# Pooling sums one unit at a time instead of two, under another list of departures from the planner's rule

## The chip, the cores and the metric

The kernel runs on one core of a Trainium2 chip. The metric is the device time of one execution in microseconds. Three runs of the kernel before gave 328.3, 327.56 and 328.4 us; the median is 328.3. Engines are named as in the profile: PE is TensorE (matrix products), DVE is VectorE, ACT is ScalarE, POOL is GpSimd, SP is the queue that issues most of the transfers.

## The reference

`x` has 4 batches of 12544 rows of 128 numbers; `inducing` has 32 rows of 128. Two attention steps are followed by a maxout layer:

```python
def mab(q, kv):
    s = scale * (q @ kv.transpose(0, 2, 1))
    s = s - s.max(-1, keepdims=True)
    a = np.exp(s)
    a /= a.sum(-1, keepdims=True) + 1e-09
    return a @ kv
h = mab(I, x)                      # 32 pooled rows for each batch
y = mab(x, h).reshape(B * S, D)    # every row of x attends to the 32 pooled rows
h1, h2 = y @ w1, y @ w2            # 128 -> 1024, twice
out = np.maximum(h1, h2) @ w_out   # 1024 -> 128
```

## The kernel before

A batch is cut into 98 chunks of 128 rows. The kernel never forms `y`. Since `max(h1, h2) = h1 + relu(h2 - h1)`, and `y` is a softmax row times the 32 pooled rows `h`, it folds the weights into them once for each batch: `hwd = h (w2 - w1)` (32 x 1024) and `m1`, which is `h w1 w_out` with the kernel's sign (32 x 128). For every chunk the main part then does this:

- `stage` (line 591) forms the exponentials `e` of up to 16 chunks in column tiles of TensorE (four tiles of 32 columns); ScalarE takes the exp.
- A `phase` (line 978) multiplies `e` with `hwd` in row tiles (four tiles of 32 rows). It fills up to four PSUM banks. Each bank is brought to SBUF through a relu, on ScalarE (line 994) or VectorE (line 997). In place of one of the four it can hold the linear part with `m1`.
- `final_one` (line 801) is one full 128 x 128 product of a relu piece with `w_out`. A phase of four banks feeds sixteen of them. The finished group is scaled by the reciprocal of the softmax sum (line 828) and stored (line 853).

So TensorE goes back and forth between row tiles, the full array and column tiles.

Beside this the pooled rows of batches 1 to 3 are prepared while the batch before is in its main part (batch 0 is pooled in a first part of its own). The pooling takes the 98 chunks as six units of 16 and a rest of two. For each unit:

- `pool_scores` (line 308), in column tiles, gives scores of 512 columns; ScalarE takes the exp with a running sum into one column of the tile `es` (line 319).
- `pool_turn` (line 345) transposes the exponentials by a transfer on SP's queue.
- `pool_accum` (line 364), in column tiles, multiplies them with the rows of x; VectorE brings the 128 x 128 partial sum to the tile `hacc` (lines 395 and 397).

In the kernel before `pool_accum` is called for every second unit: 32 products of two units stand in one bank, and VectorE adds once. In the last call the rest of two chunks is added in the same bank (line 383), with products with a column of ones that put the rest's sum of exponentials in column 128; VectorE has reduced `es` into column 128 of `hacc` beforehand (line 357), so the last add completes both the sums of rows and the sum of E. Then follow

- `small_rep` (line 409): one fp32 product of the 128 x 129 tile with `repd`, which adds the four column tiles and repeats the result; VectorE takes the reciprocal of column 128 (line 412) and scales (line 414) into the f16 tile `h4`.
- `small_h` (line 439): an f16 transpose of `h4`, copied to `hT4` (line 441).
- `small_hwd` (line 473) and `small_m1` (line 493), which fold the weights.

After the last `pool_accum` of a batch POOL copies a number that depends on the finished sum (`pace`, line 164) and then issues the seven loads of the next batch's rows.

The order of all instructions is fixed when the kernel is built. A planner keeps an account of when TensorE, ScalarE and VectorE are free (`Clock`: costs such as `ck.run(0.49, "col")` or `ck.on_dve(end, 0.22)`) and of when each of the eight PSUM banks is free. At each step it takes side work, column work, a phase or one output product. The small jobs carry a due time in finished chunks (`at`) and a condition (`ready`). The list `DEV` names steps at which the planner departs from its rule: 1 puts a phase off by one product, 2 takes a phase sooner, 3 takes no column work before a phase at this step, 4 takes column work sooner. If the account foresees that TensorE would wait, `keep_busy` puts in products without effect (line 758).

Of the kernel before, what the change touches and what calls it, by code (L numbers as in the profile page):

```python
# [102 lines left out]
def kernel(  # L103
# [56 lines left out]
    def load_x(b, i, after=None):  # L160
        k0, n = parts[b][i]
        if after is not None:

            nc.gpsimd.tensor_copy(out=pace, in_=after)  # L164
        nc.gpsimd.dma_start(out=xn_at[b, i][:, 0:n, :], in_=xr[b, :, k0 : k0 + n, :])  # L165
# [31 lines left out]
    with tc.manual_schedule(engines={ET.PE, ET.DVE, ET.Activation, ET.Pool, ET.SP}):  # L197
# [99 lines left out]
        def xn_of(b, k):  # L297
            for i, (k0, n) in enumerate(parts[b]):
                if k0 <= k < k0 + n:
                    return xn_at[b, i][:, k - k0, :]  # L300

        def pool_scores(b, u):
            if u == 0:
                st[b]["es"] = smp.tile([128, NU], F32, name=f"es_{b}", tag="esu")
            bi, ps = bank([128, 512])
            ck.wait(ck.bank[bi], "p1")
            for g in range(4):
                nc.tensor.matmul(  # L308
                    out=ps[32 * g : 32 * (g + 1), :],
                    lhsT=inducingT,  # L310
                    rhs=xT_tiles[b % 2][:, U * u + 4 * g : U * u + 4 * (g + 1), :],
                    start=True,
                    stop=True,
                    tile_position=(0, 32 * g),
                    skip_group_check=True,
                )
            end = ck.run(0.226, "col")
            eu = etp.tile([128, 512], F16, name=f"eu_{b}_{u}", tag="eu", bufs=NEU)
            nc.scalar.activation(  # L319
                out=eu, in_=ps, func=AF.Exp, scale=scale, accum_out=st[b]["es"][:, u : u + 1]  # L320
            )
            ck.bank[bi] = ck.on_act(end, 0.65)
            st[b]["eu", u] = eu, ck.bank[bi]
# [22 lines left out]
            st[b]["eT", u] = eT, ck.pe  # L346

        def pool_accum(b, u):

            bi, ps = bank([128, 512])  # L350
            ck.wait(ck.bank[bi], "p1")
            last = u == NU - 1
            if u == 1:
                st[b]["hacc"] = smp.tile([128, C + 1], F32, name=f"hacc_{b}", tag="hacc")
            acc = st[b]["hacc"]
            if last:
                nc.vector.reduce_sum(out=acc[:, C : C + 1], in_=st[b]["es"], axis=AX.X)
                ck.on_dve(st[b]["eu", u][1], 0.1)
            for v in (u - 1, u):
                eT = st[b]["eT", v][0]  # L360
                st[b]["sum", v] = True
                for j in range(4):
                    for g in range(4):
                        nc.tensor.matmul(  # L364
                            out=ps[32 * g : 32 * (g + 1), 0:128],
                            lhsT=eT[:, j, 32 * g : 32 * (g + 1)],
                            rhs=xn_of(b, U * v + 4 * g + j),
                            start=(j == 0 and v < u),
                            stop=(j == 3 and v == u and not (last and g < REST)),
                            tile_position=(0, 32 * g),  # L370
                            skip_group_check=True,
                        )
            if last:
                et = st[b]["et"][0]
                for g in range(4):
                    pairs = [(warm[:, 0:M], ones16[:, 0:1], 128, 1)]
                    if g < REST:
                        pairs = [
                            (et[:, g, :], xn_of(b, U * NU + g), 0, 128),
                            (et[:, g, :], ones16[:, 0:1], 128, 1),  # L380
                        ]
                    for lhsT, rhs, lo, n in pairs:
                        nc.tensor.matmul(
                            out=ps[32 * g : 32 * (g + 1), lo : lo + n],
                            lhsT=lhsT,
                            rhs=rhs,
                            start=False,
                            stop=True,
                            tile_position=(0, 32 * g),
                            skip_group_check=True,  # L390
                        )
            end = ck.run(0.58 if last else 0.49, "col")
            n = C + 1 if last else C
            if u == 1:
                nc.vector.tensor_copy(out=acc[:, 0:n], in_=ps[:, 0:n])
            else:
                nc.vector.tensor_add(out=acc[:, 0:n], in0=ps[:, 0:n], in1=acc[:, 0:n])  # L397
            ck.bank[bi] = ck.on_dve(end, 0.22)
            if last:
                st[b]["esrr"] = ck.bank[bi]  # L400
            if last and b + 1 < B:
                for i in range(7):
                    load_x(b + 1, i, acc[:, C : C + 1] if i == 0 else None)

        def small_rep(b):

            bi, ps = bank([128, 512])
            ck.wait(ck.bank[bi], "p1")
            nc.tensor.matmul(out=ps[:, 0 : C + 1], lhsT=repd, rhs=st[b]["hacc"], start=True, stop=True)  # L409
            end = ck.run(0.28)  # L410
            rec = smp.tile([128, 1], F32, name=f"rec_{b}", tag="rec")
            nc.vector.reciprocal(out=rec, in_=ps[:, C : C + 1])
            h4 = smp.tile([128, C], F16, name=f"h4_{b}", tag="h4")
            nc.vector.tensor_scalar(out=h4, in0=ps[:, 0:C], scalar1=rec, scalar2=None, op0=ALU.mult)
            st[b]["h4"] = h4
            ck.bank[bi] = st[b]["haccr"] = ck.on_dve(end, 0.45)

        def small_h(b):
            hT4 = smp.tile([C, 4, M], F16, name=f"hT4_{b}", tag="hT4")
            if b == 0:  # L420


                nc.vector.tensor_scalar(
                    out=hT4,
                    in0=st[0]["hps"][:, None, 0:M].broadcast_to((C, 4, M)),
                    scalar1=DOWN,
                    scalar2=None,
                    op0=ALU.mult,
                )
                st[b]["hT4r"] = ck.on_dve(st[0]["end"], 0.3)  # L430
                ck.bank[st[0]["hb"]] = st[b]["hT4r"]
                es = smp.tile([128, 1], F32, name="es_0", tag="es")
                nc.scalar.copy(out=es, in_=st[0]["eps"][:, 0:1])
                ready = ck.on_act(st[0]["end"], 0.2)
                st[b]["hT4"] = hT4.rearrange("c q m -> c (q m)")
                return es, ready
            bi, ps = bank([128, 128], F16)
            ck.wait(ck.bank[bi], "p1")
            nc.tensor.transpose(ps[:, 0:128], st[b]["h4"], identity16)
            end = ck.run(0.056)  # L440
            nc.vector.tensor_copy(out=hT4.rearrange("c q m -> c (q m)"), in_=ps[:, 0:128])
            ck.bank[bi] = st[b]["hT4r"] = ck.on_dve(end, 0.2)
            st[b]["hT4"] = hT4.rearrange("c q m -> c (q m)")
# [434 lines left out]
        def want_linear():  # L878
# [12 lines left out]


        DEV = {
            31: 1, 54: 1, 107: 2, 141: 1, 148: 1, 177: 4, 201: 1, 231: 1, 268: 1, 285: 1, 289: 1, 297: 2,
            308: 3, 310: 4, 331: 1, 339: 4, 357: 4, 358: 4, 366: 1, 375: 1, 397: 1, 409: 1, 446: 3, 457: 1,
            463: 4, 465: 3, 488: 1, 518: 2, 542: 3, 567: 4, 612: 3, 653: 1, 752: 1, 805: 1, 810: 2, 829: 1,
            834: 4, 842: 1, 846: 1, 863: 1, 900: 1, 920: 4, 946: 1, 950: 1, 966: 1, 1005: 1, 1025: 1, 1050:
            2, 1111: 1, 1119: 1, 1138: 1, 1152: 1, 1163: 1, 1190: 1, 1201: 1, 1282: 1, 1294: 1, 1299: 1,
            1301: 4, 1349: 4, 1362: 3, 1363: 2, 1370: 4, 1379: 1, 1396: 2, 1435: 1, 1459: 1, 1469: 1, 1472:
            3, 1519: 1, 1534: 1, 1536: 3, 1543: 4, 1572: 3, 1606: 1, 1617: 4, 1635: 1, 1654: 3, 1686: 1,  # L900
            1701: 3, 1729: 1
        }
        LIMIT = -16

# [107 lines left out]
        for b in range(1, B):  # L1012
            base = DONE0[b - 1]
            t_first, t_step = (6, 2.2) if b == 1 else (-6, 3.4)
            for u in range(NU):
                if b == 1:
                    s, turn, acc = 25 + 5 * u, 45 + 1.5 * u, 55 + 2 * u
                else:
                    s = turn = 13 + 8.2 * u
                    acc = s + 12  # L1020
                at(base + int(s), pool_scores, b, u)
                at(base + int(turn), pool_turn, b, u)
                if u % 2:
                    at(base + int(acc), pool_accum, b, u)
            s, end = int(s), base + int(acc)
            at(base + s + 2, pool_rest, b)
            at(end, small_rep, b)
# [165 lines left out]
```

## Time and profile before

| | |
|---|---|
| median of three runs | 328.3 us |
| the profiled execution | 328.3 us |
| its span, first to last instruction | 326.2 us |
| PE busy | 320.8 us, 5404 products |
| DVE busy | 282.3 us |
| ACT busy | 281.8 us |
| POOL busy | 25.4 us |
| output products (line 801) | 217.9 us, 3136 products |
| phases (line 978) | 88.7 + 38.8 us in two groups, 1261 products |
| pooling sums (line 364) | 5.5 us, 288 products |
| small_rep (line 409) | 1.3 us, 3 products of two passes each |

Busy time is the union of an engine's instructions; matmuls overlap, so the mean of one is longer than the distance to the next. The first 32 us or so are the first part (loading, pooling of batch 0, folding of its weights); the main part takes nearly all the rest.

### The profile page before, as it was taken

The page shows a single profiled execution, that of the slowest core. Times are in us where ns is not written, and L with a number is a line of the kernel's source. Part 1 is how long each engine was busy: PE and PEld are TensorE (multiplying, and loading weights), DVE is VectorE, ACT ScalarE, POOL GpSimd, SP SyncE. Part 2 cuts the span into 40 slices and gives each one's busy share as a digit, 9 for nine tenths or more (in the row PEclk, how much of TensorE's full clock was granted, in tenths as well). Part 3 has the DMA queues.
Part 4 walks back from the last instruction along what each step waited for, and adds up shares of the span by engine and source line. Part 5 has one row for each costly group of instructions (what it writes and reads, how often), then busy time and mean ns, then how long its engine had stood idle before and what let it go on. Part 6 is the DMA issues. An engine that isn't in the chain of part 4 may idle for free.

```text
span 326.2 us, 12587 instructions
## 1 busy us (share of the span) xinstructions
PE 320.8 (98%) x5404; PEld 243.0 (74%) x5404; DVE 282.3 (87%) x518; ACT 281.8 (86%) x564; POOL 25.4 (8%) x51
## 2 busy tenths in 40 slices
PE   8999999999999999999999999999999999999996
PEld 3886777677777777777777777777777777778785
DVE  2459998998989999999989989898999999989873
ACT  3679899999978999999988999899979999999961
POOL 7351030000040000000040000000000000000000
PEclk9999999999999999999999999999999999999999
DMA  8999999954289999983479999992422212222233
GB/s 206 209 205 213 289 235 210 228 157 131 98 170 243 191 271 200 196 180 120 111 137 239 219 254 211 191 199 81 133 97 96 86 66 100 98 98 98 87 112 112
DMA packets 70823, 53.65 MB, mean 164 GB/s; under 512 B 52176, under 2 KB 55408, under 8 KB 70768
## 3 DMA queue, kind: packets, MB, share of 16 engines
q1 hardware_dynamic: 64656, 38.63, 49.1%
q0 software_dynamic: 6112, 14.22, 22.3%
q8 instruction: 42, 0.69, 0.9%
q14 instruction: 13, 0.11, 0.1%
HBM read 28.33 MB, written 25.69 MB: 166 GB/s over the span
## 4 chain that ended last, share of the span: by engine, by line
PE 98%; ACT 0%; issue 0%; DVE 0%; ACTq 0%
PE ps L801 61%; PE ps L978 23%; PE ps L591 3%; PE ps L232 2%; PE ps L364 1%; PE ps L308 1%; PE ps L657 1%; PE ps L248 1%; PE ps L280 1%; PE ps L631 1%; PE ps L649 1%; PE ps L758 1%; PE ps L271 1%; PE ps L473 0%; PE ps L409 0%
## 5 line engine op out<-in xcount | busy, mean ns | idle before, releaser
L994 ACT ACTIVATE relu<-ps 128x512 f16<-128x512 f32 x465 | 245.3, 605 | 25.3 <-PE ps L978 16.2
L997 DVE TENSOR_SCALAR relu<-ps 128x512 f16<-128x512 f32 x319 | 204.9, 682 | 19.8 <-PE ps L978 18.3
L801 PE MATMUL ps<-woutp,relu 128*128 128x128 f16 x3136 | 217.9, 220 | 0.1
L801 PEld LDWEIGHTS <-relu 128*128 128x128 f16 x3136 | 177.0, 98 | 40.7 <-issue 30.1
L978 PE MATMUL ps<-e,hwd 32*128 32x512 f16 (+2 forms) x880 | 88.7, 360 | 0.0
L828 DVE TENSOR_TENSOR o<-ps,rp 128x512 f32<-128x512 f32 (+3 forms) x108 | 68.5, 634 | 5.7 <-PE ps L801 3.4
L978 PEld LDWEIGHTS <-hwd 32*128 32x128 f16 x880 | 24.6, 91 | 20.9 <-issue 0.8
L978 PE MATMUL ps<-m,e 32*128 32x128 f16 x381 | 38.8, 217 | 0.0
L978 PEld LDWEIGHTS <-e 32*128 32x128 f16 x381 | 21.3, 92 | 2.6
L165 POOL DMA_DIRECT2D xn<-in_x_dram x31 | 16.7, 551 | 8.4 <-DMA xn<-in_x_dram 4.5
L236 DVE COPY xT<-ps 128x512 f16<-128x512 f16 (+3 forms) x11 | 5.5, 504 | 8.2 <-PE ps L232 8.1
L603 ACT ACTIVATE e<-ps 128x512 f16<-128x512 f32 (+2 forms) x21 | 11.6, 570 | 0.0
L319 ACT ACTIVATE eu<-ps 128x512 f16<-128x512 f32 x18 | 10.8, 617 | 0.0
L591 PE MATMUL ps<-xT,hT 128*32 128x512 f16 (+3 forms) x114 | 10.1, 366 | 0.0
L164 POOL COPY pace<-hacc 128x1 f32<-128x1 f32 x2 | 0.4, 183 | 116.2 <-DVE hacc L397 116.2
L239 ACT COPY xT<-ps 128x768 f16<-128x768 f16 (+3 forms) x11 | 6.1, 556 | 3.5 <-PE ps L232 3.3
L232 PE MATMUL ps<-identity,xn 128*128 128x128 f16 x98 | 7.8, 226 | 0.1
L232 PEld LDWEIGHTS <-xn 128*128 128x128 f16 x98 | 6.0, 101 | 1.5 <-DVE xn L653 0.9
L257 ACT ACTIVATE et<-ps 128x448 f16<-128x448 f32 (+4 forms) x11 | 4.5, 413 | 2.6 <-PE ps L248 2.6
L641 DVE RECIPROCAL rp<-ps 128x16 f32<-128x16 f32 (+2 forms) x28 | 6.7, 239 | 0.0
L631 PE MATMUL ps<-ones_q,e 128*128 128x4 f16 x102 | 6.6, 166 | 0.0
L591 PEld LDWEIGHTS <-hT 128*32 128x32 f16 x114 | 2.6, 93 | 5.1 <-issue 4.2
(96 smaller groups left out, 112.6 us busy)
## 6 DMA issues: line engine op xcount, KB each, us to landing
out_dram<-o SPq DMA_DIRECT2D x90, 256.0 KB, 2.5
xn<-in_x_dram POOLq DMA_DIRECT2D x24, 448.0 KB, 12.0
out_dram<-o SPq DMA_DIRECT2D x10, 128.0 KB, 3.4
xn<-in_moe_w_dram POOLq DMA_DIRECT2D x4, 256.0 KB, 13.8
xn<-in_x_dram POOLq DMA_DIRECT2D x4, 224.0 KB, 10.2
xT<-xn SPq DMA_TRANSPOSE x42, 3.6
xf<-in_x_dram SPq DMA_DIRECT2D x1, 512.0 KB, 3.6
xf<-in_x_dram SPq DMA_DIRECT2D x1, 384.0 KB, 4.0
```

Of the source, the lines that this page charges most:

```text
L165: nc.gpsimd.dma_start(out=xn_at[b, i][:, 0:n, :], in_=xr[b, :, k0 : k0 + n, :])
L232: nc.tensor.transpose(ps[:, j, :], xn[:, g + j, :], identity16)
L319: nc.scalar.activation(out=eu, in_=ps, func=AF.Exp, scale=scale, accum_out=st[b]["es"][:, u : u + 1])
L591: nc.tensor.matmul(out=ps[32 * q : 32 * (q + 1), 128 * t : 128 * (t + n)], lhsT=hq, rhs=xT[:, c : c + n, :], start=True, stop=True, tile_p ...
L603: nc.scalar.activation(out=blk.e2[:, 0 : 128 * wd], in_=ps[:, 0 : 128 * wd], func=AF.Exp, scale=st[0]["rs"] if blk.b == 0 else scale,)
L631: nc.tensor.matmul(out=ps[:, 4 * t : 4 * t + 4], lhsT=blk.e2[:, 128 * t : 128 * (t + 1)], rhs=ones_q, start=True, stop=True,)
L641: nc.vector.reciprocal(out=blk.rp[:, 0:wd, :].rearrange("p t q -> p (t q)"), in_=ps[:, 0 : 4 * wd])
L801: nc.tensor.matmul(out=g.ps[:, 128 * c : 128 * (c + 1)], lhsT=g.blk.relu[q][:, 128 * (jb * w4 + t) : 128 * (jb * w4 + t + 1)], rhs=woutp[: ...
L828: nc.vector.tensor_mul(osb[:, 0:n, :], g.ps[:, 0 : n * C].rearrange("p (s c) -> p s c", s=n), rp)
L978: nc.tensor.matmul(**seq[i])
L994: nc.scalar.activation(out=dst, in_=src, func=AF.Relu)
L997: nc.vector.tensor_scalar(out=dst, in0=src, scalar1=0.0, scalar2=None, op0=ALU.max)
```

## The change

Three things change together.

First, `pool_accum` is called for every unit: 16 products, one bank, and one copy or add on VectorE each, so 18 calls in place of 9. Each is booked in the planner's account with 0.26 us of TensorE and 0.2 of VectorE.

Second, the sum of E is kept apart from the sums of rows. `es` gets a seventh column and is cleared by POOL. The rest's sum is copied from the bank into it on 64 partitions, and only then `es` is reduced into a new tile `esr`. `small_rep` multiplies only this one column with `repd`; VectorE takes the reciprocal and scales `hacc` in place, in fp32. `small_h` is an fp32 product of `hacc` with `repd`, which adds the four column tiles and transposes in one. The products of a column of ones with the cleared tile `warm` go.

Third, `DEV` lists 84 steps in place of 81, at other places.

```diff
         def pool_scores(b, u):
             if u == 0:
-                st[b]["es"] = smp.tile([128, NU], F32, name=f"es_{b}", tag="esu")
+                st[b]["es"] = smp.tile([128, NU + 1], F32, name=f"es_{b}", tag="esu")
+                nc.gpsimd.memset(st[b]["es"], 0.0)
...
         def pool_accum(b, u):
-
             bi, ps = bank([128, 512])
             ck.wait(ck.bank[bi], "p1")
+            eT = st[b]["eT", u][0]
+            st[b]["sum", u] = True
             last = u == NU - 1
-            if u == 1:
-                st[b]["hacc"] = smp.tile([128, C + 1], F32, name=f"hacc_{b}", tag="hacc")
-            acc = st[b]["hacc"]
-            if last:
-                nc.vector.reduce_sum(out=acc[:, C : C + 1], in_=st[b]["es"], axis=AX.X)
-                ck.on_dve(st[b]["eu", u][1], 0.1)
-            for v in (u - 1, u):
-                eT = st[b]["eT", v][0]
-                st[b]["sum", v] = True
-                for j in range(4):
-                    for g in range(4):
-                        nc.tensor.matmul(
-                            out=ps[32 * g : 32 * (g + 1), 0:128],
-                            lhsT=eT[:, j, 32 * g : 32 * (g + 1)],
-                            rhs=xn_of(b, U * v + 4 * g + j),
...
+            for j in range(4):
+                for g in range(4):
+                    nc.tensor.matmul(
+                        out=ps[32 * g : 32 * (g + 1), 0:128],
+                        lhsT=eT[:, j, 32 * g : 32 * (g + 1)],
+                        rhs=xn_of(b, U * u + 4 * g + j),
+                        start=(j == 0),
+                        stop=(j == 3 and not (last and g < REST)),
...
             if last:
                 et = st[b]["et"][0]
-                for g in range(4):
-                    pairs = [(warm[:, 0:M], ones16[:, 0:1], 128, 1)]
...
+                for g in range(REST):
+                    for rhs, lo, n in ((xn_of(b, U * NU + g), 0, 128), (ones16[:, 0:1], 128, 1)):
...
-            end = ck.run(0.58 if last else 0.49, "col")
-            n = C + 1 if last else C
-            if u == 1:
-                nc.vector.tensor_copy(out=acc[:, 0:n], in_=ps[:, 0:n])
+            end = ck.run(0.26, "col")
+            if u == 0:
+                st[b]["hacc"] = smp.tile([128, C], F32, name=f"hacc_{b}", tag="hacc")
+                nc.vector.tensor_copy(out=st[b]["hacc"], in_=ps[:, 0:128])
             else:
-                nc.vector.tensor_add(out=acc[:, 0:n], in0=ps[:, 0:n], in1=acc[:, 0:n])
-            ck.bank[bi] = ck.on_dve(end, 0.22)
+                acc = st[b]["hacc"]
+                nc.vector.tensor_add(out=acc, in0=ps[:, 0:128], in1=acc)
+            ck.bank[bi] = ck.on_dve(end, 0.2)
             if last:
-                st[b]["esrr"] = ck.bank[bi]
-            if last and b + 1 < B:
-                for i in range(7):
-                    load_x(b + 1, i, acc[:, C : C + 1] if i == 0 else None)
+                es = st[b]["es"]
+                nc.vector.tensor_copy(out=es[0 : 32 * REST, NU : NU + 1], in_=ps[0 : 32 * REST, 128:129])
+                esr = smp.tile([128, 1], F32, name=f"esr_{b}", tag="esr")
+                nc.vector.reduce_sum(out=esr, in_=es, axis=AX.X)
+                st[b]["esr"] = esr
+                ck.bank[bi] = st[b]["esrr"] = ck.on_dve(end, 0.2)
+                if b + 1 < B:
+                    for i in range(7):
+                        load_x(b + 1, i, esr if i == 0 else None)
 
         def small_rep(b):
-            nc.tensor.matmul(out=ps[:, 0 : C + 1], lhsT=repd, rhs=st[b]["hacc"], start=True, stop=True)
-            end = ck.run(0.28)
+            nc.tensor.matmul(out=ps[:, 0:1], lhsT=repd, rhs=st[b]["esr"], start=True, stop=True)
+            end = ck.run(0.11)
...
-            nc.vector.reciprocal(out=rec, in_=ps[:, C : C + 1])
-            h4 = smp.tile([128, C], F16, name=f"h4_{b}", tag="h4")
-            nc.vector.tensor_scalar(out=h4, in0=ps[:, 0:C], scalar1=rec, scalar2=None, op0=ALU.mult)
-            st[b]["h4"] = h4
-            ck.bank[bi] = st[b]["haccr"] = ck.on_dve(end, 0.45)
+            nc.vector.reciprocal(out=rec, in_=ps[:, 0:1])
+            acc = st[b]["hacc"]
+            nc.vector.tensor_scalar(out=acc, in0=acc, scalar1=rec, scalar2=None, op0=ALU.mult)
+            ck.bank[bi] = st[b]["haccr"] = ck.on_dve(end, 0.4)
 
         def small_h(b):
...
-            bi, ps = bank([128, 128], F16)
+            bi, ps = bank([128, 512])
             ck.wait(ck.bank[bi], "p1")
-            nc.tensor.transpose(ps[:, 0:128], st[b]["h4"], identity16)
-            end = ck.run(0.056)
+            nc.tensor.matmul(out=ps[:, 0:128], lhsT=st[b]["hacc"], rhs=repd, start=True, stop=True)
+            end = ck.run(0.25)
             nc.vector.tensor_copy(out=hT4.rearrange("c q m -> c (q m)"), in_=ps[:, 0:128])
...
         DEV = {
-            31: 1, 54: 1, 107: 2, 141: 1, 148: 1, 177: 4, 201: 1, 231: 1, 268: 1, 285: 1, 289: 1, 297: 2,
...
+            0: 1, 27: 1, 32: 1, 35: 2, 52: 1, 87: 2, 157: 3, 168: 1, 169: 4, 181: 2, 244: 2, 247: 1, 397: 4,
...
                 at(base + int(s), pool_scores, b, u)
                 at(base + int(turn), pool_turn, b, u)
-                if u % 2:
-                    at(base + int(acc), pool_accum, b, u)
+                at(base + int(acc), pool_accum, b, u)
```

## The prediction

> **What bounds the kernel now.** I read the page first: busy shares, chain that ended last, groups; then the order of the instructions of both programs; then what each engine waited for; then stretches of the main part; then single moments around the pooling.
>
> ```profile
> PE 320.8 (98%) x5404; PEld 243.0 (74%) x5404; DVE 282.3 (87%) x518; ACT 281.8 (86%) x564; POOL 25.4 (8%) x51
> ...
> PEclk9999999999999999999999999999999999999999
> ...
> PE 98%; ACT 0%; issue 0%; DVE 0%; ACTq 0%
> ...
> L994 ACT ACTIVATE relu<-ps 128x512 f16<-128x512 f32 x465 | 245.3, 605 | 25.3 <-PE ps L978 16.2
> L997 DVE TENSOR_SCALAR relu<-ps 128x512 f16<-128x512 f32 x319 | 204.9, 682 | 19.8 <-PE ps L978 18.3
> ```
>
> TensorE is the chain: 98% of it, at full clock in all 40 slices. ScalarE and VectorE wait for TensorE (the 16.2 and 18.3 us behind the relus), hardly the other way round. Matmul ends are modelled, so I did not trust the 98% alone and took the distance from one matmul's start to the next. In the main part it is clockwork: 0.056 us between output products (line 801), 0.152 from a product to the first matmul of a phase (so 0.096 for a change of tiling), 0.327 for nearly every phase. Summing everything above the usual distance of its kind leaves 2.4 us of stalls in the whole program, and only 0.78 us after 35 us: 0.09 each at 73.9 and 79.2, 0.16 at 89.4, 0.10 at 166.2, 0.16 at 247.3 and five under 0.05. So the time is the sum of TensorE's work, and a change pays or costs what it adds to that sum plus the stalls it makes.
>
> ```profile
> 33.00:60.00 27.00, 27.00 (x425) 19.80 (x421) 24.79 (x42) 25.72 (x52) 2.55 (x2) 1.00 1.12 236
> ...
> 85.00:110.00 25.00, 25.00 (x438) 18.76 (x435) 23.01 (x46) 21.14 (x41) 3.93 (x8) 1.00 0.87 194
> ...
> 230.00:260.00 30.00, 30.00 (x514) 23.07 (x512) 28.52 (x58) 26.16 (x51) 0.00 (x0) 1.00 0.29 95
> ```
>
> After the stretch, its length and TensorE come weight loads, VectorE (the fifth figure) and ScalarE. VectorE is 92 to 95% full in these stretches: free on average, but a short chain on it stands behind relus of 0.68 us.
>
> **The change, part by part.** The profiled execution took 328.3 us (span 326.2), which is also the median of the runs shown, so the sum is made against 328.3.
>
> (1) The number of tiling changes. Nine sums of two units become eighteen sums of one. If each new one opened its own visit to column tiles, that would be 9 x 2 x 0.096 = 1.7 us. The instruction order says otherwise: sums of one unit are put beside each other or beside a staging. Visits to column tiles are 33 before and 34 after, all changes of tiling 481 and 482, row stretches 222 and 222, products 3136 and 3136, fillers 13 and 13. Cost: +0.1. That is also all the new list of 84 steps (81 before) does to the sum. It moves phases and columns by a few products, and the spacing of phases is nearly the same (two phases after a phase: median 2.42 us of work in both orders, least 2.09 and 2.07).
>
> The Trainium skill has a rule that speaks against this part ("TensorEngine Tiling (Array Packing)", Key Properties): a change of tiling mode drains TensorE. The row agrees, 0.152 against 0.056. By the rule with one mode change in and one out for each added sum it would be the 1.7 above; by the counted visits it is 0.1, and the count decides.
>
> (2) TensorE work of the small steps.
>
> ```profile
> L409 PE MATMUL ps<-hacc,repd 128*128 128x129 f32 x6 | 1.3, 306 | 0.0
> ...
> L439 PE MATMUL ps<-identity,h 128*128 128x128 f16 x3 | 0.7, 223 | 0.0
> ...
> L449 PE MATMUL ps<-es,rep 128*128 128x1 f32 x2 | 0.3, 236 | 0.0
> ```
>
> Durations overlap, so I take starts. The fp32 product of 129 columns (line 409) holds TensorE 0.166 + 0.112 = 0.278 us; an fp32 product of one column (line 449) twice 0.084 = 0.168; the f16 transpose 0.059. Now small_rep takes one column (-0.11) and small_h takes an fp32 product of 128 columns in place of the transpose (+0.22): +0.11, three times +0.33. Two products of ones less in each last sum: about -0.1 in all. The sums' 288 products are unchanged. Parts 1 and 2 together: +0.3.
>
> (3) The chain from the last sum to small_rep. Before, the sum of E is reduced ahead of the last add, and the product with ones sits in the same bank, so one add finishes both.
>
> ```profile
> 88.51 0.22 PE L383 MATMUL ps<-xn,et 128*32 128x128 f16 x2
> ...
> 88.91 0.15 DVE L357 TENSOR_REDUCE hacc<-es 128x1 f32<-128x6 f32 x1
> ...
> 89.17 0.29 DVE L397 TENSOR_TENSOR hacc<-ps,hacc 128x129 f32<-128x129 f32 x1
> ...
> 89.61 0.46 PE L409 MATMUL ps<-hacc,repd 128*128 128x129 f32 x2
> ```
>
> From the add's start to small_rep are 0.44 us here, where small_rep waited 0.16 for it. In the other two pooled batches the add stood 0.50 and 0.63 us behind the first line-383 product (here 0.66) and nothing was late. After the change add, copy of the ones column and reduce follow each other: 0.21 from the add to the copy (as from the add at 163.76 to the next VectorE start), 0.26 from the copy to the reduce that reads it (as from this reduce to this add), 0.15 for the reduce, 0.15 to TensorE: 0.77. The planner gives small_rep in the three batches 11, 8 and 10 products after the last sum (6, 9 and 10 before). At 0.056 a product, the 0.94, 1.11 and 1.16 us between them (without the stall) become 1.22, 1.05 and 1.16. With the add where it stood, small_rep can start at 1.43, 1.27 and 1.40: late by 0.21, 0.22 and 0.24, together 0.67, of which 0.16 is there already. So +0.5. If the add comes earlier by the 0.26 of the reduce no longer ahead of it, nothing is late: -0.16. If a relu (0.68) slips in ahead each time it is up to +2.5. I take +0.5, since the add must wait for a relu under way in any case. Behind a waiting small_rep stand the next products and the next phase, so its lateness is lost whole. The pacing copy on POOL waits for the same reduce, then the seven loads. Their tiles are needed no earlier than the next batch's transposes, which stand tens of products further on, so 0.3 us there costs nothing; without that cover it would be the 0.3.
>
> (4) small_h to small_hwd. The fp32 product ends 0.22 later than the transpose, and its fp32 bank is copied in about 0.29 (line 504: 292 ns) in place of 0.22. Against +0.29 the planner gives +0.43, +0.59 and -0.06 us. In the third batch, where the weights' product already started 0.10 after the copy, it can be late by 0.35. I take +0.15, half, because the copy's place between relus is not known; ends 0 and +0.35. Scaling moves from a bank (line 414: 351 ns) to a tile in SBUF (nearest line 672: 219 ns): -0.13 on VectorE in a chain that has room, counted as nothing.
>
> The skill ("VectorE: DVE Perf Modes", the table of perf-mode tiers) likewise puts fp32 tensor_scalar from SBUF a tier above one from PSUM; no run yet shows this instruction. An estimate from that page, half of 351 ns, would give the chain 0.17 us and leave the sum as it is.
>
> (5) VectorE's load. Nine more adds and copies at 0.29 (+2.6), three small copies (+0.45), the copies of fp32 banks (+0.2), scaling (-0.4), and two relus that the planner moves from ScalarE (+1.3): about +4 us, of 23 free between 33 and 318 us. Its own planner books 0.20 a sum where the row has 0.29. The relus behind a sum come late by that much, and a phase or product behind them can wait. Before, the stalls beside nine sums (79.2, 85.3 and the like) are 0.13 to 0.22 us; twice as many sums make +0.2. Ends: -0.2 (they vanish) and 9 x 0.29 = +2.6 (every added sum is paid by TensorE).
>
> (6) Costed at nothing: the memset of the E sums on POOL, 0.1 us by the 128x1 memsets (101 ns). POOL has nothing from 44 us to 89.5 and then only the loads, done within 5 us, and each pool_scores comes 30 us or more behind them. Were POOL late, the exp that accumulates into the tile would hold ScalarE for as long. SP's queue: two transposes of E and one store change places with a neighbour, all else is in its old order.
>
> Sum: 0.3 + 0.5 + 0.15 + 0.2 = +1.15 us, 329.4 us (+0.35%).
>
> **The rivals.** A measurement of this kernel can tell about 0.3% (1.0 us) from no change.
>
> A. Not slower: the add comes earlier because no reduce stands ahead of it, so the longer chain fits its gaps. The place is the three small_rep products; the price left is parts 1 and 2, +0.3, so 328.6 us, 328.1 to 329.3. It decides if the add starts within about 0.4 us of the line-383 products. For it: the whole stall budget after 35 us is 0.78 us, and the planner places the new order with the same slack. Against it: already one of three was late before, with a chain 0.33 shorter.
>
> B. Faster: shorter sums free bank and VectorE sooner, and all 0.78 us of stalls goes: 328.3 + 0.3 - 0.8 = 327.8 us. Even that is within 0.3%; to pass it, work would have to leave TensorE, and the counts show none leaving.
>
> C. Much slower: VectorE, at 95% in places, turns into the bound there, so each added sum costs its 0.29: 0.3 + 0.5 + 2.6 = +3.4, 331.7 us. For it: relus on both engines keep eight banks turning at 92 to 95%. Against: the sums of before stood in the same stretches almost unpaid.
>
> D. The change does nothing to the order: excluded, TensorE's order differs from 31.6 us on.
>
> **How the numbers follow.** Forecast 0.47 (329.3 to 330.6), A 0.38, B 0.06 in all (0.05 of it beyond 0.3%), C 0.09. Slower by over 0.3%: the forecast nearly whole, and C: 0.55. Faster: 0.05. Same: 0.40. The range drops B and the top of C: 328.1 to 331.0.
>
> **What would show it.** Parts 1 and 2: TensorE's busy time up by about as much as the span, 5400 instructions within ten, tiling changes at 0.152 still. Part 3: the fp32 products of small_rep late by 0.2 us each behind the reduce. Part 4: a late weights' product in the last batch. Part 5: VectorE near 286 us busy, its wait behind phases (18.3) smaller. I am wrong if a stall of over 0.5 us stands anywhere else (a staging, a transpose of x that comes late), or if TensorE's sum moved by over 0.5 us.

## The result and the profile after

The changed kernel takes 329.74 us (median of 6 runs, 329.04 to 330.07). The kernel before took 327.82 us beside it (6 runs, 327.49 to 328.4). The ratio is 1.0055, 95% interval 1.0039 to 1.0070: about 1.8 us slower. The profiled execution took 329.54 us, its span is 327.6 us.

The first lines are the head of the page of the changed kernel, then the chain that ended last and the two relu groups (lines 985 and 988 are 994 and 997 of the kernel before).

```profile
PE 321.6 (98%) x5401; PEld 243.8 (74%) x5401; DVE 284.8 (87%) x532; ACT 281.0 (86%) x562; POOL 25.8 (8%) x54
...
PE 94%; DVE 2%; ACT 1%; DMA 1%; issue 1%; DVEq 0%; ACTq 0%
...
L985 ACT ACTIVATE relu<-ps 128x512 f16<-128x512 f32 x463 | 244.8, 603 | 28.9 <-PE ps L969 20.6
L988 DVE TENSOR_SCALAR relu<-ps 128x512 f16<-128x512 f32 x321 | 205.6, 681 | 18.2 <-PE ps L969 17.3
```

TensorE is still the chain, with 94% of it in place of 98%. Some of the difference is in the start. In the main part it is in the stretches with pooling, where TensorE was busy all the time before (length, TensorE, weight loads, VectorE, ScalarE and so on):

```profile
33.00:60.00 27.00, 27.00 (x431) 19.94 (x428) 24.84 (x42) 25.72 (x52) 2.59 (x3) 1.00 1.13 238
85.00:110.00 25.00, 24.85 (x412) 18.62 (x409) 22.78 (x47) 20.63 (x40) 4.04 (x9) 1.00 0.95 208
230.00:260.00 30.00, 29.87 (x507) 22.85 (x505) 28.15 (x59) 25.59 (x50) 0.00 (x0) 1.00 0.30 102
```

The stretch before the first pooling sums (33 to 60) is full as ever. The other two lack 0.15 and 0.13 us of TensorE, and a start that comes late while an earlier matmul still shows as running is not even counted there. In the last one the place is small_rep (0.13 idle before 239.66 us); in the middle one it is small_rep (0.07 before 87.57) and a pooling sum (0.08 before 85.78). The longest wait is in the second pooled batch, outside these stretches. This is VectorE there in the changed kernel, and then TensorE in the same microseconds:

```profile
162.51 0.68 DVE L988 TENSOR_SCALAR relu<-ps 128x512 f16<-128x512 f32 x1
163.10 0.68 DVE L385 TENSOR_TENSOR hacc<-ps,hacc 128x128 f32<-128x128 f32 x2
163.70 0.14 DVE L389 COPY es<-ps 64x1 f32<-64x1 f32 x1
163.94 0.16 DVE L391 TENSOR_REDUCE esr<-es 128x1 f32<-128x7 f32 x1
```

```profile
162.79 0.22 PE L370 MATMUL ps<-xn,et 128*32 128x128 f16 x2
...
163.77 0.23 PE L792 MATMUL ps<-woutp,relu 128*128 128x128 f16 x1
164.24 0.35 PE L401 MATMUL ps<-esr,repd 128*128 128x1 f32 x2 [0.24 <-DVE esr L391]
```

Between the product at 163.77 and small_rep at 164.24 lie 0.47 us where 0.07 is usual. Two adds, a copy and a reduce follow each other, and small_rep waits for the last of them.

To see where the whole difference stands I summed the distances from one product's start to the next by kind in both traces. From the first folding product (line 469, 23.13 us before; line 460, 22.97 after) to the end are 303.05 and 304.60 us, so +1.55 us. The parts, rounded, with the little that falls on the edges left out:

| from one product's start to the next | before | after | difference |
|---|---|---|---|
| into small_rep, three times | 0.36 | 1.13 | +0.77 |
| small_rep itself | 0.85 | 0.65 | -0.20 |
| small_h itself | 0.18 | 0.83 | +0.65 |
| into small_h | 0.29 | 0.18 | -0.11 |
| column tiles, with entry and exit | 25.19 | 25.71 | +0.52 |
| products, and from a product into a phase | 195.84 | 195.56 | -0.28 |
| inside phases, and out of them | 67.53 | 67.78 | +0.25 |

Two rows need more detail.

*Column tiles.* One of the edges left out is an exit of the kernel before from column tiles into another small product (0.15 us, at 154.52); counted in, column work grew by 0.37. Another 0.15 of it is a phase that is now entered from column tiles and no longer from a product, which the row of products saves. So about 0.2 is new. The rest of what the row of products saves, 0.16, is the stall at 247.3 us of the kernel before, which does not come back.

*Phases.* The +0.25 is not spread over them. From the first matmul of a phase to what follows it, the 191 phases that lead back to products take 63.56 us before and 63.55 after; the 27 that lead into column tiles take 8.81 and 9.01. Nearly all of these 0.20 us are one place, the pooling sum at 85.78 us, which starts 0.19 late. VectorE ahead of it, and then TensorE:

```profile
81.66 1.07 DVE L385 TENSOR_TENSOR hacc<-ps,hacc 128x128 f32<-128x128 f32 x3
82.65 1.88 DVE L988 TENSOR_SCALAR relu<-ps 128x512 f16<-128x512 f32 x3
84.44 0.68 DVE L819 TENSOR_TENSOR o<-ps,rp 128x512 f32<-128x512 f32 x1
85.04 1.88 DVE L988 TENSOR_SCALAR relu<-ps 128x512 f16<-128x512 f32 x3
```

```profile
85.78 0.41 PE L357 MATMUL ps<-xn,eT 128*32 128x128 f16 x16
```

VectorE has no pause from three adds in a row on. The first product of the sum waits for VectorE and starts 0.05 us after the relu that began at 85.04 has ended (85.72). That the added adds pushed this relu back is argued from the order; no run takes them away.

The first part before the folding differs by chance, which is taken up at the end. So each kernel below has, beside its ratio, this time from the first folding product to the end in its profiled execution ("main time", 303.05 before, 304.60 after).

### The profile page after: what moved, and what is told of

Same layout as the page of the kernel before. It is cut to its first block, busy times and chain, and to the rows that moved or that the text cites. A ratio compares the mean times of both kernels' runs of the same rounds, so it can differ in the third digit from the quotient of the medians.

```text
span 327.6 us, 12592 instructions
## 1 busy us (share of the span) xinstructions
PE 321.6 (98%) x5401; PEld 243.8 (74%) x5401; DVE 284.8 (87%) x532; ACT 281.0 (86%) x562; POOL 25.8 (8%) x54
## 4 chain that ended last, share of the span: by engine, by line
PE 94%; DVE 2%; ACT 1%; DMA 1%; issue 1%; DVEq 0%; ACTq 0%
PE ps L792 60%; PE ps L969 22%; PE ps L582 3%; PE ps L232 2%; PE ps L357 1%; PE ps L309 1%; DMA xf<-in_x_dram 1%; PE ps L248 1%; ACT relu L985 1%; DVE relu L988 1%; PE ps L280 1%; PE ps L622 1%; PE ps L749 1%; PE ps L271 1%; PE ps L640 0%
```

## The experiments

Theory S: the extra time is the longer chain to small_rep and the fp32 products, with some column work and phases late behind the added adds. Rival L: the list, or the one-unit sums with their load on VectorE, make it. In the first four kernels the numbers of the planner's account were left as they were, so that TensorE's order is that of the kernel they start from, but for the small products.

### old_small: the changed kernel with the old small steps

```diff
 # in the changed kernel
+            if last:
+                nc.vector.reduce_sum(out=acc[:, C : C + 1], in_=st[b]["es"], axis=AX.X)
...
+                nc.vector.tensor_add(out=acc[:, 0:n], in0=ps[:, 0:n], in1=acc[:, 0:n])
...
-            nc.tensor.matmul(out=ps[:, 0:1], lhsT=repd, rhs=st[b]["esr"], start=True, stop=True)
+            nc.tensor.matmul(out=ps[:, 0 : C + 1], lhsT=repd, rhs=st[b]["hacc"], start=True, stop=True)
...
-            nc.tensor.matmul(out=ps[:, 0:128], lhsT=st[b]["hacc"], rhs=repd, start=True, stop=True)
+            nc.tensor.transpose(ps[:, 0:128], st[b]["h4"], identity16)
```

> The changed kernel with the small steps of the kernel before put back: sum of E reduced ahead of the last add, one add of 129 columns, small_rep of 129 columns, f16 transpose. The sums stay one unit at a time, the list of departures and the planner's account are those of the changed kernel, so TensorE's order stays except for the small products. Theory S (the extra time is the longer chain to small_rep, 0.93 us of lateness in the trace of the changed kernel, and the fp32 small products, about +0.3 us of TensorE work; the rest, some 0.5 us, is column work): about 1.1 us less than the changed kernel, a ratio to the kernel before of about 1.002, and no lateness over 0.2 us in front of small_rep. Rival L (the list, or the sums of one unit and their load on VectorE, make the time): the ratio stays at 1.0045 or more.

Measured: ratio 1.0031 (1.0019 to 1.0042), main time 303.98, 0.62 us under the changed kernel and 0.93 above the kernel before. The step into small_rep falls from 1.13 to 0.58 us, small_h from 0.83 to 0.17, while small_rep itself takes 0.24 more. But 0.4 us comes back: the distances inside phases and out of them grow from 67.78 to 68.16, most of it in two phases behind small_h that are taken up under h_f16. So the small steps are a part of the cost and not all of it. L's 1.0045 is excluded; S put the gain at 1.1 us and had not seen the giving back.

### new_small: the kernel before with the new small steps

```diff
 # in the kernel before
-                nc.vector.reduce_sum(out=acc[:, C : C + 1], in_=st[b]["es"], axis=AX.X)
...
+                nc.vector.tensor_copy(out=es[0 : 32 * REST, NU : NU + 1], in_=ps[0 : 32 * REST, 128:129])
+                nc.vector.reduce_sum(out=esr, in_=es, axis=AX.X)
...
+            nc.tensor.matmul(out=ps[:, 0:1], lhsT=repd, rhs=st[b]["esr"], start=True, stop=True)
...
+            nc.tensor.matmul(out=ps[:, 0:128], lhsT=st[b]["hacc"], rhs=repd, start=True, stop=True)
```

> The kernel before with the small steps of the changed kernel alone (E kept in its own tile, copy and reduce behind the last add, fp32 small_h); sums of two units, the list and the planner's account are those of the kernel before. Theory S: small_rep late by about 0.5, 0.2 and 0.25 us in the three batches, in place of 0.16 in all, and +0.33 us of products: about +1.1 us, a ratio of 1.0033. Rival L: a ratio within 0.001 of 1.

Measured: ratio 1.0020 (1.0011 to 1.0029), main time 303.89, +0.84. S is nearer than L, but its 1.1 us (1.0033) was too much, and the place was wrong: small_rep is hardly later (0.41 us for the three in place of 0.36). VectorE in the first pooled batch of new_small shows why:

```profile
88.32 0.28 DVE L391 TENSOR_TENSOR hacc<-ps,hacc 128x128 f32<-128x128 f32 x1
88.52 0.14 DVE L395 COPY es<-ps 64x1 f32<-64x1 f32 x1
88.76 0.16 DVE L397 TENSOR_REDUCE esr<-es 128x1 f32<-128x7 f32 x1
```

The first product of the rest stands at 87.92 us, so the add starts 0.40 us behind it (0.28 and 0.39 in the other batches), as early as if the reduce ahead of it had simply gone. From the add to small_rep (89.07) are 0.75 us, the 0.77 of the prediction. The chain is as long as thought and fits. In the changed kernel the same add starts 0.83, 0.70 and 0.70 us behind. In its second and third batch the sums of units 4 and 5 stand in one visit to column tiles, and the add of unit 5 must wait for that of unit 4 (the "x2" at 163.10 above; the second starts 0.38 after the first). The cost here is small_h: +0.69 for the fp32 products and +0.35 for its lateness in the second and third batch, less 0.24 for the shorter small_rep. In the second batch the profile puts the wait of small_h down to a relu on ScalarE:

```profile
166.12 0.46 PE L436 MATMUL ps<-repd,hacc 128*128 128x128 f32 x2 [0.20 <-ACT relu L991]
```

### e_first: the E chain ahead of the add

```diff
 # in the changed kernel
+                if last:
+                    nc.vector.tensor_copy(out=es[0 : 32 * REST, NU : NU + 1], in_=ps[0 : 32 * REST, 128:129])
+                    nc.vector.reduce_sum(out=esr, in_=es, axis=AX.X)
                 nc.vector.tensor_add(out=acc, in0=ps[:, 0:128], in1=acc)
...
-                nc.vector.tensor_copy(out=es[0 : 32 * REST, NU : NU + 1], in_=ps[0 : 32 * REST, 128:129])
-                nc.vector.reduce_sum(out=esr, in_=es, axis=AX.X)
```

> The changed kernel with one thing moved: on VectorE the copy and the reduce of E stand ahead of the last add in place of behind it. TensorE's order is unchanged. Theory S: small_rep needs the reduce alone and comes 0.2 to 0.3 us sooner in each batch, 0.6 to 0.8 us in all, so a ratio to the kernel before of about 1.0035. Rival V (VectorE is late anyway, the chain's order doesn't matter): the ratio of the changed kernel, 1.0055.

Measured: ratio 1.0016 (1.0007 to 1.0025), main time 303.66, 0.94 under the changed kernel, more than the 0.6 to 0.8 (and 1.0035) of S. VectorE and then TensorE in the second pooled batch of e_first:

```profile
162.66 0.14 DVE L387 COPY es<-ps 64x1 f32<-64x1 f32 x1
162.91 0.16 DVE L389 TENSOR_REDUCE esr<-es 128x1 f32<-128x7 f32 x1
162.98 0.28 DVE L391 TENSOR_TENSOR hacc<-ps,hacc 128x128 f32<-128x128 f32 x1
```

```profile
163.13 0.23 PE L793 MATMUL ps<-woutp,relu 128*128 128x128 f16 x1
163.21 0.35 PE L402 MATMUL ps<-esr,repd 128*128 128x1 f32 x2
```

small_rep follows its product in 0.08 us. Laid beside the trace of the changed kernel, product by product, the two stay level except at the three small_reps, where e_first gains 0.19, 0.39 and 0.29 us and keeps all of it. That one chain, three times on VectorE, was half of the cost of the whole change (0.77 of 1.55 us of main time); e_first gains more than that because it also takes away 0.11 of lateness that the kernel before had.

### h_f16: small_h in f16

```diff
 # in the changed kernel
+                nc.vector.tensor_copy(out=repd16, in_=repd)
...
-            nc.vector.tensor_scalar(out=acc, in0=acc, scalar1=rec, scalar2=None, op0=ALU.mult)
+            nc.vector.tensor_scalar(out=h4, in0=st[b]["hacc"], scalar1=rec, scalar2=None, op0=ALU.mult)
...
-            nc.tensor.matmul(out=ps[:, 0:128], lhsT=st[b]["hacc"], rhs=repd, start=True, stop=True)
+            nc.tensor.matmul(out=ps[:, 0:128], lhsT=st[b]["h4"], rhs=repd16, start=True, stop=True)
```

> The changed kernel with small_h in f16: VectorE writes the scaled sums as f16, and the product uses an f16 copy of repd (made once at the start). TensorE's order is unchanged. Theory S: three fp32 products of 0.28 us become 0.06, so 0.65 us less, a ratio of about 1.0035; small_hwd is nowhere late. Rival: the fp32 product hides in time that TensorE would lose anyway, and the ratio stays at 1.0055.

Measured: ratio 1.0045 (1.0033 to 1.0057), main time 304.34, only 0.26 under the changed kernel: between S and its rival. small_h fell from 0.83 to 0.17 us as expected. In the first two batches, the phase about 1 us later took back 0.17 and 0.15 us. ScalarE and the phase of the changed kernel in the first batch, and then those of h_f16:

```profile
89.59 1.09 ACT L985 ACTIVATE relu<-ps 128x512 f16<-128x512 f32 x2 [1.10 <-PE ps L969]
...
90.76 0.40 PE L969 MATMUL ps<-e,hwd 32*128 32x256 f16 x6
```

```profile
89.67 1.08 ACT L988 ACTIVATE relu<-ps 128x512 f16<-128x512 f32 x2 [1.10 <-PE ps L972]
...
90.61 0.56 PE L972 MATMUL ps<-e,hwd 32*128 32x256 f16 x6
```

The first folding product stands at 22.97 us in the changed kernel and at 23.06 in h_f16. Counted from there the phase starts 0.23 us sooner and takes 0.17 longer, so the next product (91.09 and 91.11) comes only 0.06 sooner. A phase needs four banks, and one is not free: the fourth matmul starts at 90.81, waits for ScalarE, and the second of ScalarE's two relus ended at 90.76. In the second batch the late matmul starts at 167.28, and a relu of ScalarE ended at 167.23. Counted from the first folding product these relus end at the same time in both kernels, to 0.02 us: ScalarE got this work from a phase ahead of small_h, and a shorter small_h does not hurry it. Another 0.08 us comes back in steps too small to name.

### split_adds: more adds in the kernel before

```diff
 # in the kernel before: the second unit of a pair goes to columns 128..255 of the same bank
-                            out=ps[32 * g : 32 * (g + 1), 0:128],
+                            out=ps[32 * g : 32 * (g + 1), lo2 : lo2 + 128],
...
+            if not last:
+                nc.vector.tensor_add(out=acc[:, 0:128], in0=ps[:, 128:256], in1=acc[:, 0:128])
```

> The kernel before with the second unit of a pair summed into columns 128 to 255 of the same bank and brought in by an add of its own, in the first two calls of each batch: six more adds of 0.29 us on VectorE, TensorE's order and the bank use unchanged. Theory S, in which VectorE's extra adds are hidden by its free time: ratio to the kernel before within 0.0007 of 1, and the products after the sums no later than before. Rival V (every added sum is paid by TensorE, because the relus behind it are late): 6 x 0.29 = 1.7 us, a ratio of 1.005.

Measured: ratio 1.0037 (1.0024 to 1.0049), main time 303.97, +0.92 us. Both theories miss: the added adds are not hidden, and not paid whole. Laid beside the kernel before, the time goes in four places: 0.11, 0.33, 0.31 and 0.18 us, each inside the first phase behind a sum. One of them, in the lines of split_adds:

```profile
214.98 0.29 DVE L400 TENSOR_TENSOR hacc<-ps,hacc 128x128 f32<-128x128 f32 x1
215.00 0.10 PEld L981 LDWEIGHTS <-hwd 32*128 32x128 f16 x3
215.00 0.71 PE L981 MATMUL ps<-e,hwd 32*128 32x512 f16 x4
215.32 0.09 PEld L981 LDWEIGHTS <-hwd 32*128 32x128 f16 x1 [0.22 <-DVE hacc L400]
```

The fourth matmul of the phase waits for the added add itself: the planner gave it the bank of the sum, which in its account is free after one add. The first two places (0.11 and 0.33) are of the same kind: the matmul starts 0.06 us behind the end of an added add. The fourth (0.18) is of the kind that V names: there the added add pushes a relu back, and the matmul starts 0.05 us after this relu has ended. So an add behind a sum is paid mostly when the next phase gets the sum's bank (0.75 of the 0.92 us) and only once through a late relu. The other two adds show no place of their own; on average it is 0.15 us an add.

### pairs_e_first_h_f16 and e_first_h_f16: the repairs together

The first is the kernel before with its pairs, and the small steps of the two kernels above (E chain ahead of the add, one column in small_rep, f16 small_h). The second is the changed kernel with both repairs.

```diff
 # pairs_e_first_h_f16, in new_small
+            if last:
+                nc.vector.tensor_copy(out=es[0 : 32 * REST, NU : NU + 1], in_=ps[0 : 32 * REST, 128:129])
+                nc.vector.reduce_sum(out=esr, in_=es, axis=AX.X)
             if u == 1:
...
-            nc.tensor.matmul(out=ps[:, 0:128], lhsT=st[b]["hacc"], rhs=repd, start=True, stop=True)
+            nc.tensor.matmul(out=ps[:, 0:128], lhsT=st[b]["h4"], rhs=repd16, start=True, stop=True)
 # e_first_h_f16: the diffs of e_first and of h_f16
```

> The kernel before, with its sums of two units, list and account, and with the small steps in a third form: E in its own tile with copy and reduce ahead of the last add, small_rep of one column, small_h as an f16 product. TensorE's order is that of the kernel before. Theory S: small_rep is 0.11 us shorter three times and its lateness of 0.16 us goes: 0.3 to 0.5 us less than the kernel before, a ratio of 0.9985 to 0.999, if nothing of it is given back. Rival G (time taken out of a small step is given back at the next phase, which waits for its banks, as the look at h_f16 suggests: 0.17 and 0.15 us returned behind small_h in two of three batches): a ratio of 0.9995 to 1.0005.

> The changed kernel with both repairs: copy and reduce of E ahead of the last add, and small_h in f16. Theory S: 0.90 us (as in e_first's trace) and 0.66 us, of which about 0.3 is given back, so 1.2 us less than the changed kernel: a ratio to the kernel before of 1.0005 to 1.0015. Rival: the two add up whole, and with 1.55 us less the ratio is 0.9995 or below it.

Measured: 1.0003 (0.9994 to 1.0013) with a main time of 302.92, and 1.0031 (1.0019 to 1.0042) with 303.58. In the first, small_rep with the way to it takes 0.37 us less (0.84 in place of 1.21), and 0.17 of that comes back at once as lateness of small_h in the second batch; the time is that of the kernel before. That is the number of G and not its place: small_h waits there for the scaled sums on VectorE (0.29 us, line 414), and not a phase for its banks. In the second, the f16 product again saves 0.67 us, and beside e_first nearly all of it comes back: 0.17 and 0.15 in the phases as in h_f16, 0.13 into the weights' product of the third batch, the rest in small steps. Its main time is level with e_first (303.66). So S, which put the two repairs at 1.0005 to 1.0015, missed, as did its rival; the ratio lies above e_first's, which the trace does not explain. No kernel here beats the kernel before.

### The lists

Four kernels keep everything but `DEV`: each kernel with the other's list, and each with none. (Their instruction orders differ widely, so the parts of their time are not compared one by one.)

```diff
 # before_other_list: the kernel before with the changed kernel's DEV; after_other_list the reverse
 # before_no_list, after_no_list
-        DEV = {
...
+        DEV = {}
```

> The kernel before under the list of 84 steps of the changed kernel; nothing else. The instruction order then has 485 changes of tiling in place of 481 and as many fillers. Theory S (a list belongs to the order that it was made for; elsewhere its steps are noise that costs some changes of tiling): 4 x 0.1 plus the drains and stalls around them, 0.4 to 1.0 us, a ratio of 1.001 to 1.003. Rival L (the list of the changed kernel is itself what makes it slower, or what is good in it): a ratio of 1.005 or more, or below 1.

> The kernel before with an empty list of departures. 484 changes of tiling in place of 481. After before_other_list (2.0 us more than the kernel before outside the first part, by its trace) theory S says that a list is worth something only in the order that it was made for: without one the kernel should lie between, 0.5 to 1.5 us slower than with its own, a ratio of 1.0015 to 1.0045. Rival: the steps of a list hardly matter in themselves, and the other list cost what it did by chance; ratio within 0.001 of 1.

> The changed kernel with an empty list: against before_no_list it shows what the sums of one unit and the new small steps cost where neither order was adjusted. 485 changes of tiling. Theory S (late small_rep 0.8, small_h 0.65, phases behind more adds 0.25, less small_rep 0.2): 1.2 to 1.8 us slower than before_no_list, a ratio to the kernel before of 1.006 to 1.009. Rival L (the difference of the two kernels is that of their lists): as fast as before_no_list.

> The changed kernel under the list of 81 steps of the kernel before. 487 changes of tiling in place of 482. Theory S (a list is noise in another order): 0.5 to 2 us slower than the changed kernel, a ratio to the kernel before of 1.007 to 1.012. Rival L (the list of the kernel before is the better one by itself): faster than the changed kernel, a ratio under 1.005.

| | own list | other list | no list |
|---|---|---|---|
| kernel before | 1 | 1.0067 (1.0054 to 1.0079) | 1.0073 (1.0061 to 1.0085) |
| changed kernel | 1.0055 (1.0039 to 1.0070) | 1.0081 (1.0069 to 1.0093) | 1.0082 (1.0069 to 1.0095) |

A list in the other kernel is worth nothing: the time is that of no list. Its own list is worth about 2.4 us to the kernel before and 0.9 us to the changed kernel. Both are more than the three to five changes of tiling that the instruction orders count (0.5 us at most, at 0.096 each). S had expected less for the kernel before: up to 1.003 with the other list, up to 1.0045 with none. And without lists the two kernels stand 0.1% apart, within the noise of both ratios, where S expected 1.2 to 1.8 us. By this table the two kernels differ mostly in what their lists bring.

That does not take the cost of the small steps away. Without lists the steps into small_rep are 0.76 us in the kernel before and 1.16 in the changed one, small_rep itself 0.92 and 0.64, into small_h 0.18 and 0.18, small_h itself 0.17 and 0.83: together +0.78 us, where the two kernels with their lists have +1.11. Something else makes up for it.

The trace of before_no_list has one cause that can be named. It is the first line of its waits of TensorE, and the issues of the transposes of x on SP's queue:

```profile
PE ps L308 <- DMA xT<-xn: 1.4, 1, 1.4
```

```profile
107.34 6.07 SPq L171 DMA_TRANSPOSE xT<-xn  x1
```

A score product stood 1.4 us for a transpose of x, whose issue came behind one that took 6.07 us. The kernel before with its list has no such wait in its main part. Less this wait, the two kernels without lists would differ by about 1.6 us by the ratios and 1.1 by the main times (305.78 and 305.50), near what S expected, and its list would be worth 1.0 us to the kernel before, no more than to the changed one. Whether the wait repeats was the last question.

```diff
 # in before_no_list
-                return d.get(("T", (U * a[1] + U - 1) // (P1 // 2)), INF) + 8.0 <= now
+                return d.get(("T", (U * a[1] + U - 1) // (P1 // 2)), INF) + 10.0 <= now
```

> before_no_list with one number changed: the planner lets scores follow the transposes of x by 10 us in place of 8. In the trace of before_no_list the last product of a visit to column tiles stood 1.5 us for a transpose of x, because one issue on SP's queue took 6.07 us where 1.3 is usual. Theory S: this one wait is what lifts before_no_list to the level of after_no_list; without it 0.9 to 1.9 us less, a ratio to the kernel before of 1.0015 to 1.0045, so that without lists the changed sums and small steps cost 1 to 2 us as they do with lists. Rival L: the wait is an accident of one execution, and the ratio stays at 1.006 or more.

Measured: 1.0077 (1.0065 to 1.0089). The edit left TensorE's order exactly as it was, so it took nothing away. What it shows is a repeat, with the wait in it again:

```profile
PE ps L308 <- DMA xT<-xn: 1.3, 1, 1.3
```

So it is no accident of one execution, and it belongs to that order. That without it the two would stand 1.1 to 1.6 us apart is arithmetic; a kernel without it was not run, so how much of the 1.8 us belongs to the lists stays open.

## Why the prediction was right, point by point

The forecast was +1.15 us on 328.3, 329.4 us, slower by over 0.3% at 0.55; measured were 329.74 us and about +1.8. Direction and range held. That the time came nearer than the difference is luck: the sum started from 328.3, and the kernel before took 327.82 in six runs. Part of the agreement is errors that cancel: parts 1 to 3 came out about 0.6 us larger than forecast, part 4 did not come (0.15), and two stalls of the kernel before, 0.10 at 166.2 and 0.16 at 247.3, did not come back.

- Bound. Right: TensorE's work and stalls make the time. The lateness at small_rep was lost whole (e_first gets all of it back); time taken out of small_h was mostly given back.
- Parts 1 and 2, tilings and small products (+0.3). The products came out at +0.45 (small_rep -0.20, small_h +0.65; forecast -0.33 and +0.66). The one-column product of small_rep takes more of its place than the two starts at line 449 led to think. Column work took about +0.2, where the forecast had nothing left after the products of ones. Together +0.7, so this term was undersized by 0.4.
- Part 3, small_rep (+0.5). The right place and mechanism, undersized: +0.77 in the trace. The length of the chain was right (0.77 forecast, 0.75 measured). The relu under way that I named put the add late in the first batch alone (the relus from 85.64 us on). In the other two it was the add of unit 4 directly ahead, which comes from the very grouping that part 1 counted as a saving.
- Part 4, small_hwd (+0.15). It did not come: the step into its first product is 0.19 us for the three batches, against 0.17 before. The scaling in SBUF took 0.29 us (line 406) in place of 0.35, so neither the 0.13 that the prediction took off nor its estimate of 0.17 us came, without effect on the sum.
- Part 5, VectorE (+0.2). The size is right, +0.25 inside phases and out of them, and VectorE was busy for 284.8 us, near the 286 named. The mechanism is seen in one place, the sum at 85.78 us behind a late relu (0.19 us), and not behind twice as many sums. That the size came out is in part luck: split_adds shows another way to pay, a phase that waits for the sum's bank itself.
- "That is also all the new list does to the sum" was wrong as an account of lists. The counts of tilings were right, but a list is worth 0.9 and 2.4 us in its own kernel (1.4 of the 2.4 is one wait for a transpose of x), and counts don't show that. What I compared were two adjusted orders, in which that worth was already included.
- Rival A lost by part 3: the add had to start within 0.4 us of the rest's products, and started 0.70 to 0.83 behind. In new_small it did start within 0.40, and small_rep was on time. Rivals B and C did not occur; 0.25 us for nine adds is far from the 2.6 of C; of the 0.78 us of stalls that B wanted gone some went (the two named above), but others came.

## What to carry to other kernels

When the bound engine runs like clockwork, price a change by the distance from start to start on it, and look at each place where it waits for a short chain on another engine: the order of four instructions of 0.15 to 0.3 us there was worth 0.9 us, where the whole change cost 1.55 of main time. Time taken out in front of a resource that comes free at a fixed moment is given back: of the 0.66 us of fp32 products that h_f16 removed, 0.26 stayed. A list of adjustments belongs to the order it was made for and should be made again after a change of the work; carried over it was worth nothing here.

## What the runs showed that I had not expected

The first part varies from run to run by more than most effects here. Below are the first eight transposes of the kernel before and of e_first in their profiled executions. TensorE's order up to there is the same.

```profile
5.17 1.03 PE L232 MATMUL ps<-identity,xn 128*128 128x128 f16 x8
6.00 0.89 PE L649 MATMUL ps<-warm 128*128 128x512 f16 x2
```

```profile
5.26 0.62 PE L232 MATMUL ps<-identity,xn 128*128 128x128 f16 x8
5.71 0.59 PE L641 MATMUL ps<-warm 128*128 128x512 f16 x2
```

From the first transpose to the next kind of product are 0.83 us in one and 0.45 in the other, 0.104 and 0.056 us a transpose. The first folding product stands at 23.13 and 22.54 us. The granted clock is 1.00 in the stretch 5.0 to 6.5 us of both. The Trainium skill ("TensorE: Matmul & The Clock Gate", What you observe) describes such a step, from about 107 to 56 ns a product, at a moment that varies by 500 ns either way from run to run. The distances agree; the granted clock in the profile does not show it, so that this step is the cause is argued from the distances. That is why I compared the kernels from the first folding product on.
